# Block 0's first four feature tiles in two half blocks, a shorter weight conversion, and the first weights loaded first

## The chip, the cores and the metric

The kernel runs on one core of a Trainium2 chip. The metric is the device time of one launch in microseconds (us). Before the change it is 537.87 us, the median of three runs (537.53 to 538.58).

## What is computed

Three layers follow each other: a chunked state-space attention, a gated feed-forward layer, and a second feed-forward layer with a softmax-weighted activation.

```python
# attention, per chunk of the sequence (state starts at zero)
L = exp(cum_i - cum_j) * causal;  M = (C @ B.T) * L
y = M @ x + (C @ state) * exp(cum)
state = exp(sum(log_a)) * state + sum_j B_j x_j exp(cum_end - cum_j)
# gated layer: 3072 tokens, 256 -> 1536 -> 256
xn = x / sqrt(mean(x*x) + 1e-6) * rms_g
x  = (silu(xn @ w_gate) * (xn @ w_val)) @ w_out
# second layer: 256 -> 1024 -> 256
h = x @ w_in;  solu = h * softmax(h)
out = (solu - mean) / sqrt(var + 1e-6) * g_ln @ w_out2
```

The kernel takes the weights as the 64-bit floats that they are on the host and makes 32-bit ones of them itself.

## The kernel before, in words

**Units and blocks.** The 3072 tokens are 24 units of 128 tokens, six to each of four sequences. Four units make a block (`BLOCKS`, line 27); block 0 holds the first unit of every sequence. A unit goes through the attention (`at_...`), a block through the gated layer (`g_gate`, `g_val`, `o_mm`, lines 634 to 692), and each unit through the second layer (`m_...`).

**A unit of the attention.** `ld_bc` (line 220) and `ld_xb` (231) load it. For units 0 to 3 `at_lpe` (275) and `at_lpx` (283) make the decay matrix, `at_cb` (304) multiplies C by B, `at_mt` (314) multiplies the two on VectorE, and `at_y` (379, 384) gives the output in PSUM. Then the output is normalised: `at_sq` squares it on ScalarE (408), `at_ms` sums over partitions on TensorE (414), `at_ts` (427) and `at_pw` (432) make the inverse root, `at_rb` spreads it with a transpose against `ident` (436), `at_xc` copies the output to SBUF on ScalarE (442), `at_xn` multiplies by the gain and the inverse root on VectorE, once for each of two halves of 128 columns (447). `at_xh` (454) and `at_xl` (458) split the result into a high and a low part; `xl` ends the unit.

**The gated layer.** 1536 features are 12 tiles of 128 (`NF`). For each, `g_mm` (line 641) makes gate and value: six matmuls each (two halves of the 256 inputs, times high by high, low by high and high by low), with the block's 512 tokens as the moving columns. One PSUM bank (`pg`, `pv`) is there for each. `g_tanh` (655, ScalarE), `g_silu` (659) and `g_mul` (666, VectorE) follow. `o_mm` adds the tile into two PSUM banks `po0` and `po1`, for block 0 with one fp32 matmul per half of the outputs (686), for the others with three (689). Units 1 and 3 use `po0` and `po1` for their own products ahead of that, and the decay rows of `at_lpe` and `c_rows` (996) use `pg` and `pv`.

**Weights.** 26 pieces of 512 KB come through a ring of four staging buffers. Piece 3c is the gate weights of feature tiles 2c and 2c+1, 3c+1 the value weights, 3c+2 the output weights; the last eight are the second layer's. `w_load` (127) issues a piece on SyncE. `w_conv` makes 32-bit floats of the two 32-bit words of each number, in three operations on VectorE (135, 138, 142), `w_hi` (151, ScalarE) and `w_lo` (155, VectorE or GpSimd) split them into high and low parts.

**What sets the order.** Nothing is ordered by hand but the first instructions (lines 1136 to 1149). Every step is an `op` with an engine, a booked duration, a due time, what it comes after, and the buffers that it takes. `plan()` issues them engine by engine: among the steps that could start soonest it takes the one with the earliest due time. Each engine then runs its own list in that order. The due times come from the constants at the top (lines 28 to 53): `PRO` and `FIRST` for the start and length of block 0's gated layer, `PER` for the others, `Y0`, `YU`, `YO` for the units, `HO`, `HU` for the second layer, `EARLY` and `LEAD` for the loads. SyncE issues nearly all loads, in the planned order too.

```python
ready = [f"xl{u}" for u in range(u0, u0 + n)] if True else []
...
op(f"gm{s}", "PE", mm_us(N, 6) + 0.03, t, (g_gate, b, f), after=ready + wg_n + pr, new=[("pg", f"pg{s}")],
...
op(f"lbc{u}", "SP", 0.85, Y - 9, (ld_bc, u), new=[("bc", f"bc{u}")], kb=128)
```

So every gate of a block comes after `xl` of all its units, and a load of a unit is due a fixed time ahead of the unit.

## Time and profile before

| | before |
|---|---|
| median of the runs | 537.87 us |
| the profiled execution | 536.72 us |
| its span in the trace | 535.0 us |
| TensorE busy | 97% of the span |
| VectorE / ScalarE / GpSimd busy | 78% / 56% / 22% |
| mean granted TensorE clock | 0.990 of full speed |

The trace is of one execution; the span runs from its first to its last instruction, and the profiled execution took 1.7 us more than that. PE is TensorE, PEld its weight loads, DVE VectorE, ACT ScalarE, POOL GpSimd, SP SyncE. A name such as `pg<-xh,wg_h` says which tile is written from which.

### The profile page before, as it was taken

Reading aid. Unit: us, or ns where it says so; the run is one execution under the profiler, and the core shown is the slowest. Engines: PE = TensorE matmul, PEld = TensorE weight load, DVE = VectorE, ACT = ScalarE, POOL = GpSimd, SP = SyncE. Lnnn points to the kernel's source line nnn. Section 1 sums busy time; section 2 is a strip of 40 time slices with the busy share of each in tenths; the row PEclk is TensorE's granted clock in tenths of the full one; section 3 lists DMA queues with packets and bytes.
Section 4 is the critical chain, followed back from the end, with each engine's and each line's share of the span. In section 5 each row is a group of like instructions: output and inputs, shape, how many; then the busy total and the mean of one; then the engine's idle time right before and its main releaser. Section 6 shows DMA issues by size and latency. Waiting matters only on the chain.

```text
span 535.0 us, 9649 instructions
## 1 busy us (share of the span) xinstructions
PE 521.3 (97%) x3448; PEld 424.4 (79%) x3448; DVE 416.7 (78%) x778; ACT 301.5 (56%) x657; POOL 115.4 (22%) x147
## 2 busy tenths in 40 slices
PE   8879999999999999999999999999999999999996
PEld 8657666777878888878888888888878888888796
DVE  4889999999899897874888777797776665665674
ACT  6535544655747777763485674676534444443465
POOL 2412222531222223420131331251301000000000
PEclk9969999999999999999999999999999999999999
DMA  6672554743441643751254353253121122211200
GB/s 174 204 271 89 190 187 161 232 134 124 143 138 46 193 157 125 192 168 35 81 180 120 104 173 122 82 188 109 55 74 69 37 78 90 88 50 40 88 21 30
DMA packets 43248, 64.77 MB, mean 121 GB/s; under 512 B 7104, under 2 KB 29504, under 8 KB 43200
## 3 DMA queue, kind: packets, MB, share of 16 engines
q1 hardware_dynamic: 43200, 64.16, 38.5%
q8 instruction: 27, 0.44, 0.3%
q14 instruction: 21, 0.17, 0.1%
HBM read 50.31 MB, written 13.83 MB: 120 GB/s over the span
## 4 chain that ended last, share of the span: by engine, by line
PE 79%; DVE 10%; DMA 5%; ACT 2%; issue 2%; SPq 1%; POOL 0%; DVEq 0%; ACTq 0%; POOLq 0%
PE pg L641 16%; PE pv L641 16%; PE po L689 13%; PE pf L618 12%; PE ph L489 11%; PE po L686 3%; DMA xb<-in_xbt_dram 2%; PE y L374 2%; PE y L379 2%; PE pcb L304 1%; DMA stage<-in_wv_dram 1%; DVE wt L138 1%; PE y L414 1%; DMA stage<-in_wg_dram 1%; DVE th L659 1%
## 5 line engine op out<-in xcount | busy, mean ns | idle before, releaser
L641 PE MATMUL pg<-xh,wg_h 128*128 128x512 f32 x144 | 62.5, 434 | 1.9 <-ACT xh L454 1.2
L672 ACT ACTIVATE ah<-th 128x512 fp32r<-128x512 f32 x60 | 37.8, 629 | 47.1 <-PE po L689 31.7
L655 ACT ACTIVATE th<-pg 128x512 f32<-128x512 f32 x72 | 42.7, 593 | 30.9 <-PE pg L641 30.7
L659 DVE SCALAR_TENSOR_TENSOR th<-th,pg 128x512 f32<-128x512 f32 x72 | 49.0, 681 | 13.2 <-ACT th L655 12.9
L641 PE MATMUL pv<-xh,wv_h 128*128 128x512 f32 x144 | 58.1, 403 | 0.0
L641 PE MATMUL pg<-xl,wg_h 128*128 128x512 f32 x144 | 57.1, 397 | 0.4 <-DVE xl L458 0.4
L641 PE MATMUL pg<-xh,wg_l 128*128 128x512 f32 x144 | 57.1, 396 | 0.0
L678 DVE TENSOR_TENSOR al<-th,ah 128x512 fp32r<-128x512 f32 x56 | 41.9, 748 | 18.5 <-ACT ah L672 18.3
L641 PE MATMUL pv<-xh,wv_l 128*128 128x512 f32 x144 | 56.3, 391 | 0.0
L641 PE MATMUL pv<-xl,wv_h 128*128 128x512 f32 x144 | 56.3, 391 | 0.0
L253 ACT ACTIVATE L<-L,cneg 128x128 f32<-128x128 f32 x160 | 50.1, 390 | 3.4 <-DMA L<-crow 3.4
L618 PE MATMUL pf<-wo_h,utl 128*128 128x256 f32 x176 | 49.7, 282 | 0.6 <-DVE utl L594 0.6
L618 PE MATMUL pf<-wo_h,uth 128*128 128x256 f32 x176 | 49.6, 282 | 0.0
L618 PE MATMUL pf<-wo_l,uth 128*128 128x256 f32 x176 | 49.5, 281 | 0.0
L689 PE MATMUL po<-ah,wo_h 128*128 128x512 f32 x120 | 49.0, 408 | 0.0
L554 POOL TENSOR_TENSOR sc<-sc,mhalf 128x1 f32<-128x1 f32 x24 | 14.1, 588 | 154.9 <-DVE sc L549 154.9
L689 PE MATMUL po<-al,wo_h 128*128 128x512 f32 x120 | 47.3, 394 | 0.0
L689 PE MATMUL po<-ah,wo_l 128*128 128x512 f32 x120 | 47.3, 394 | 0.0
L666 DVE TENSOR_TENSOR th<-pv,th 128x512 f32<-128x512 f32 x60 | 41.4, 690 | 7.1 <-PE pv L641 2.0
L513 ACT ACTIVATE ut<-ph,sc 128x1024 f32<-128x1024 f32 x20 | 22.3, 1114 | 32.3 <-DVE sc L500 32.2
L489 PE MATMUL ph<-wi_h,xh 128*128 128x512 f32 x96 | 38.5, 401 | 0.3 <-DVE L L311 0.2
L489 PE MATMUL ph<-wi_h,xl 128*128 128x512 f32 x96 | 37.6, 391 | 0.2 <-DVE xl L702 0.2
(150 smaller groups left out, 1241.3 us busy)
## 6 DMA issues: line engine op xcount, KB each, us to landing
L<-crow SPq DMA_DIRECT2D x20, 512.0 KB
scr<-dt SPq DMA_DIRECT2D x20, 512.0 KB
tt<-scr SPq DMA_DIRECT2D x80, 128.0 KB
bc<-in_bcT_dram SPq DMA_DIRECT2D x48, 128.0 KB
stage<-in_wo_dram SPq DMA_DIRECT2D x10, 512.0 KB
xb<-in_xbt_dram SPq DMA_DIRECT2D x24, 192.0 KB
stage<-in_wg_dram SPq DMA_DIRECT2D x6, 512.0 KB
stage<-in_wv_dram SPq DMA_DIRECT2D x6, 512.0 KB
```

What stands on the lines that cost most here:

```text
L253: A.activation(d["L"][:, h], d["L"][:, h], AF.Exp, bias=cneg[:, R(u) * 8 + h:R(u) * 8 + h + 1])
L489: T.matmul(ph[c], xx[:, kk, k * P:(k + 1) * P], ww[:, kk, 512 * c:512 * c + 512], start=(i == 0), stop=(i == 5))
L513: A.activation(d["u"], ph[0], AF.Exp, bias=sc[:, 0:1], accum_out=sc[:, 1:2])
L618: T.matmul(d["pf"][:, 0:DM], uu[:, k], ww[:, k], start=(k == 0 and i == 0), stop=(k == 7 and i == 2))
L641: T.matmul(ps[:, :n], ww[:, kk, f * P:(f + 1) * P], xx[:, kk, :n], start=(i == 0), stop=(i == 5))
L655: A.activation(d["th"], d["pg"], AF.Tanh, scale=0.5)
L659: V.scalar_tensor_tensor(out=d["th"], in0=d["th"], scalar=1.0, in1=d["pg"], op0=ALU.add, op1=ALU.mult)
L666: V.tensor_tensor(out=out, in0=d["pv"], in1=d["th"], op=ALU.mult)
L672: A.activation(d["ah"], d["th"], AF.Copy)
L678: e.tensor_tensor(out=d["al"], in0=d["th"], in1=d["ah"].bitcast(F32), op=ALU.subtract)
L686: T.matmul(po[b, m][:, :n], w_raw(3 * (f // 2) + 2).bitcast(F32)[:, 256 * (f % 2) + m * P:256 * (f % 2) + (m + 1) * P], d["aw"], start=f == 0,
L689: T.matmul(po[b, m][:, :n], ww[:, f, m * P:(m + 1) * P], aa, start=(f == 0 and i == 0), stop=(f == NF - 1 and i == 2))
```

## The change

- The first four feature tiles of block 0 go as four half steps, numbered from `HALF` = 100. Half step `100 + 2h + j` makes feature tiles 2j and 2j+1 for units 2h and 2h+1: `h_mm` issues twelve matmuls of 256 columns for a gate, where `g_mm` issues six of 512, and puts the two tiles side by side in one bank. It comes after `xl` of its two units alone. `oh_mm` adds them to the output with two matmuls of 256 columns for each half of the outputs. From the fifth feature tile on block 0 goes as before.
- `w_conv`: the second operation was one over two tensors. Now it shifts one byte of the low word into the high word's lowest byte, in place, with byte views; the third takes its bits from the high word alone.
- `at_xc` multiplies by the gain, in two copies of 128 columns; `at_xn` is one multiplication of 256 columns. `xc` comes after `cst`, which loads the gain.
- The first two pieces are issued ahead of the plan, the first on SyncE after `aT` (the decays), the second on ScalarE's queue after `um` (the cumulation masks), which moves there from SyncE. `ident` is loaded within the plan, due at 9, and `rb` of units 0 to 3 comes after it. Loads of pieces no longer come after one another. By `EARLY` pieces 4 and 3 are due at -16.47 and -13.6, unit 0's `lbc` at 3.29 - 4.76 - 9 = -10.47.
- The constants of the due times are new, and some booked durations.

```diff
-LEAD = 17.3
-PER = (12.7, 1.36, 6.5)
+LEAD = 17.84
+PER = (12.7, 1.53, 7.29)
 WIDE = 1
+PAIRS = 2
 AHEAD = 4
-PRO = 25.1
-FIRST = 74.7
+PRO = 21.84
+FIRST = 98.91
 WARM = 7
-Y0 = (12.7, 2.9)
-YPOS = 0.58
-YSPAN = 0.85
-TAILGAP = 8.8
-SLACK = 0.15
-SLACK0 = 0.0
+Y0 = (3.29, 1.62)
+YPOS = 0.56
+YSPAN = 0.94
+TAILGAP = 12.33
+SLACK = 0.17
+SLACK0 = 0.37
...
-EARLY = (-1.0, -4.6, 2.95, 6.0)
+EARLY = (-3.25, -13.6, -16.47, 20.8)
...
-CROW = 28.3
-WGAP = 10.7
-HLAG = (52.3, 20.9)
-YO = (-2.93, 2.27, -5.8, 2.92, -2.9)
-HO = (9.9, 2.75, 0.38, 0.0, -10.0, -6.6)
-YU = (0.0, -1.59, 0.0, 0.0, 0.0, 0.0, -5.1, -5.5, 2.61, 3.5, 0.0, 0.0, 1.6, 0.0, 3.3, -7.3, 0.93, -6.4, -2.01, -0.21, 6.3, -1.89, -2.22, 0.0)
-HU = (-7.2, 0.0, 1.26, 0.0, 0.0, 0.0, 8.7, -0.65, 0.71, 0.0, 1.15, -0.74, -2.67, 1.65, -5.3, -1.89, 4.6, -1.02, 0.0, -0.82, -0.59, 8.2, 0.0, 0.0)
+CROW = 13.2
+WGAP = 13.8
+HLAG = (65.44, 23.03)
+YO = (-10.65, -4.15, -1.07, 3.02, -9.67)
+HO = (10.4, 5.84, -0.94, -3.36, -10.98, -28.16)
...
-    def w_load(i):
+    def w_load(i, e):
         src = pieces[i][1]
         t = stg[i] = sp.tile([P, 1024], I32, name="stage", tag="u", bufs=BUFS["u"])
-        S.dma_start(t.rearrange("p (k f) -> p k f", k=2), src.bitcast(I32).rearrange("(k p) f -> p k f", p=P))
+        e.dma_start(t.rearrange("p (k f) -> p k f", k=2), src.bitcast(I32).rearrange("(k p) f -> p k f", p=P))
...
         elif c == 1:
-            V.scalar_tensor_tensor(out=t, in0=v[:, :, 1], scalar=-0x40000000, in1=t, op0=ALU.bitwise_and,
-                                   op1=ALU.bitwise_or)
+            b = stg[i].bitcast(mybir.dt.uint8).rearrange("p (f w) -> p f w", w=8)
+            V.tensor_scalar(out=b[:, :, 4], in0=b[:, :, 3], scalar1=5, scalar2=None, op0=ALU.logical_shift_right)
...
             raw = w_raw(i) if pieces[i][0][0] == "o" else t
-            V.scalar_tensor_tensor(out=raw, in0=v[:, :, 0], scalar=29, in1=t, op0=ALU.logical_shift_right,
+            V.scalar_tensor_tensor(out=raw, in0=v[:, :, 1], scalar=-0x3FFFFFF9, in1=t, op0=ALU.bitwise_and,
                                    op1=ALU.bitwise_or)
...
-        A.activation(d["xts"], d["y"][:, 0:256].rearrange("p (g i) -> p g i", g=2), AF.Copy)
+        for g in range(2):
+            A.activation(d["xts"][:, g], d["y"][:, g * P:(g + 1) * P], AF.Copy, scale=rgt[:, g:g + 1])
 
     def at_xn(u):
         d = st[u]
-        for g in range(2):
-            V.scalar_tensor_tensor(out=d["xts"][:, g], in0=d["xts"][:, g], scalar=rgt[:, g:g + 1],
-                                   in1=d["y"][:, 384:512], op0=ALU.mult, op1=ALU.mult)
+        V.tensor_tensor(out=d["xts"], in0=d["xts"], in1=d["y"][:, 384:512].unsqueeze(1).to_broadcast([P, 2, P]), op=ALU.mult)
...
+    HALF = 100
...
+    def h_mm(f, ws, tag):
+        h, j = divmod(f - HALF, PAIRS)
+        ps = pp.tile([P, 512], F32, name=tag, tag=tag)
+        for q in range(2):
+            i = 0
+            for kk in range(2):
+                for xx, ww in ((xs[0][0], ws[0]), (xs[0][1], ws[0]), (xs[0][0], ws[1])):
+                    T.matmul(ps[:, 256 * q:256 * q + 256], ww[:, kk, (2 * j + q) * P:(2 * j + q + 1) * P], xx[:, kk, 256 * h:256 * h + 256],
+                             start=(q == 0 and i == 0), stop=(i == 5), skip_group_check=True)
+                    i += 1
+        act.setdefault((0, f), {})[tag] = ps
+
     def g_gate(b, f):
-        g_mm(b, f, wg_s, "pg")
+        h_mm(f, wg_s, "pg") if f >= HALF else g_mm(b, f, wg_s, "pg")
 
     def g_val(b, f):
-        g_mm(b, f, wv_s, "pv")
+        h_mm(f, wv_s, "pv") if f >= HALF else g_mm(b, f, wv_s, "pv")
...
+    def oh_mm(f, m):
+        h, j = divmod(f - HALF, PAIRS)
+        if f == HALF:
+            po[0, m] = pp.tile([P, 512], F32, name=f"po{m}")
+        for q in range(2):
+            T.matmul(po[0, m][:, 256 * h:256 * h + 256], w_raw(3 * j + 2).bitcast(F32)[:, 256 * q + m * P:256 * q + (m + 1) * P],
+                     act[0, f]["aw"][:, 256 * q:256 * q + 256], start=(f == HALF and q == 0), stop=False, skip_group_check=True)
+        if m == 1:
+            act.pop((0, f))
+
     def o_mm(b, f, m):
+        if f >= HALF:
+            return oh_mm(f, m)
...
+    FIRSTW = (S, A)
+
     def wdue(i):
         if i < 18:
             c, q = divmod(i, 3)
-            return gdue(0, 2 * c + (LAG if q == 2 else 0)) - 4.0
+            return gdue(0, (c if c < PAIRS else 2 * c) + (LAG if q == 2 else 0)) - 4.0
...
-        op(f"wl{i}", "SP", 0.45, EARLY[i] if i < len(EARLY) else t - LEAD, (w_load, i), after=[f"wl{i-1}"] if i else [], new=[("u", f"st{i}")], kb=512)
+        first = i < len(FIRSTW)
+        op(f"wl{i}", "SP", 0.0 if first else 0.45, i - 9.0 if first else EARLY[i - 2] if i < len(EARLY) + 2 else t - LEAD,
+           (int,) if first else (w_load, i, S), new=[("u", f"st{i}")], kb=512)
         for k in range(3):
-            op(f"wc{i}.{k}", "DVE", 0.41 if k == 0 else 0.68, t, (w_conv, i, k),
+            op(f"wc{i}.{k}", "DVE", 0.41 if k < 2 else 0.68, t, (w_conv, i, k),
...
+            last = [f"o{m}0.{f}" for f in ([HALF + PAIRS + c] if c < PAIRS else [2 * c, 2 * c + 1]) for m in range(2)]
...
+        steps = list(range(NF)) if b >= WIDE else list(range(HALF, HALF + 2 * PAIRS)) + list(range(2 * PAIRS, NF))
+        for g, f in enumerate(steps):
+            t = gdue(b, g)
+            to = gdue(b, g + LAG) + 2.0 if g + LAG < NF else t + 2.0 + LAG * (start[b + 1] - start[b]) / NF
             s = f"{b}.{f}"
-            pr = [f"vm{b}.{f-1}"] if f else ([f"vm{b-1}.{NF-1}"] if b else [])
-            wg_n, wv_n, wo_n = ([f"wh{3*(f//2)+q}", f"w{3*(f//2)+q}"] for q in range(3))
-            op(f"gm{s}", "PE", mm_us(N, 6) + 0.03, t, (g_gate, b, f), after=ready + wg_n + pr, new=[("pg", f"pg{s}")],
+            prev = f"{b}.{steps[g - 1]}"
+            pr = [f"vm{prev}"] if g else ([f"vm{b-1}.{NF-1}"] if b else [])
+            half = f >= HALF
+            c = (f - HALF) % PAIRS if half else f // 2
+            rdy = ready[2 * ((f - HALF) // PAIRS):][:2] if half else ready
+            wg_n, wv_n, wo_n = ([f"wh{3*c+q}", f"w{3*c+q}"] for q in range(3))
+            op(f"gm{s}", "PE", (2.6, 1.7, 1.43, 1.43)[g] if half else mm_us(N, 6) + 0.03, t, (g_gate, b, f), after=rdy + wg_n + pr, new=[("pg", f"pg{s}")],
...
+                op(f"o{m}{s}", "PE", mm_us(N, 4), to, (o_mm, b, f, m), after=[f"mu{s}", f"wc{3*c+2}.2"] + ([f"o{m}{prev}"] if g else []) + ([f"o0{s}"] if m else []),
+                   new=[(f"po{m}", f"po{m}{b}")] if g == 0 else [], use=[f"aw{s}", f"po{m}{b}", f"raw{c // 4}"])
...
+    def ld_ident():
+        S.dma_start(ident, consts[:, 3 * P:4 * P])
...
+    op("idn", "SP", 0.45, 9, (ld_ident,), kb=64)
...
-        ops[f"xn{u}"]["after"].append("cst")
+        ops[f"xc{u}"]["after"].append("cst")
+        ops[f"rb{u}"]["after"].append("idn")
...
-        SETUP = 5.2
-        free = dict(PE=SETUP, ACT=SETUP, DVE=SETUP + 0.6, POOL=SETUP, SP=2.6)
+        SETUP = 4.5
+        free = dict(PE=SETUP, ACT=SETUP, DVE=SETUP + 0.6, POOL=SETUP, SP=1.7)
...
-        S.dma_start(um, consts[:, 0:3 * P])
-        S.dma_start(ident, consts[:, 3 * P:4 * P])
+        A.dma_start(um, consts[:, 0:3 * P])
+        for i, e in enumerate(FIRSTW):
+            w_load(i, e)
```

## Rows read from the trace of the kernel before

**Rows 1.** The page, busy time of each engine.

```profile
PE 521.3 (97%) x3448; PEld 424.4 (79%) x3448; DVE 416.7 (78%) x778; ACT 301.5 (56%) x657; POOL 115.4 (22%) x147
```

**Rows 2.** Stretches, all engines: stretch, length, busy us (instructions), clock, DMA share, GB/s.

```profile
core 0: us, PE busy (x) PEld busy (x) DVE busy (x) ACT busy (x) POOL busy (x), PEclk, DMA share, GB/s
0.00:10.00 10.00, 8.49 (x58) 7.75 (x59) 3.38 (x7) 5.96 (x13) 2.07 (x8) 1.00 0.68 173
10.00:20.00 10.00, 8.67 (x119) 7.50 (x117) 7.41 (x17) 6.34 (x22) 4.20 (x8) 1.00 0.83 234
20.00:26.00 6.00, 5.12 (x61) 4.05 (x61) 5.69 (x14) 3.92 (x13) 2.89 (x4) 1.00 0.54 162
26.00:33.70 7.70, 4.59 (x33) 2.78 (x31) 6.87 (x19) 2.33 (x6) 2.63 (x3) 0.52 0.74 230
33.70:40.00 6.30, 6.30 (x21) 4.92 (x22) 5.21 (x10) 2.09 (x5) 0.00 (x0) 0.78 0.79 295
40.00:60.00 20.00, 20.00 (x137) 14.26 (x136) 18.14 (x35) 12.24 (x36) 5.09 (x5) 1.00 0.44 138
60.00:100.00 40.00, 39.73 (x290) 26.96 (x289) 38.17 (x72) 18.10 (x46) 9.82 (x10) 1.00 0.54 178
100.00:140.00 40.00, 39.37 (x293) 29.87 (x293) 37.10 (x67) 24.97 (x63) 15.16 (x18) 1.00 0.45 140
140.00:200.00 60.00, 59.73 (x403) 48.70 (x404) 54.41 (x95) 39.75 (x86) 14.89 (x21) 1.00 0.45 139
200.00:400.00 200.00, 198.87 (x1311) 166.53 (x1310) 153.52 (x284) 123.09 (x262) 51.23 (x64) 1.00 0.40 120
520.00:535.00 15.00, 10.66 (x89) 10.21 (x87) 7.07 (x24) 7.14 (x17) 1.64 (x3) 0.99 0.08 28
```

**Rows 3.** The same stretch, gate and value matmuls (line 641) alone: PE, PEld.

```profile
26.00:33.70 7.70, 0.79 (x1) 0.29 (x1) 0.52 0.74 230
```

**Rows 4.** Timeline, VectorE, low parts of units 1 and 3: start, us, instruction.

```profile
25.47 0.42 DVE L458 TENSOR_TENSOR xl<-xts,xh 128x256 fp32r<-128x256 f32 x1
...
33.23 0.42 DVE L458 TENSOR_TENSOR xl<-xts,xh 128x256 fp32r<-128x256 f32 x1
```

**Rows 5.** Chain that ended last, 0 to 110 us: start, us, what.

```profile
33.70 2.50 PE pg L641 x5
...
40.65 0.86 PE po L686 x2
41.50 1.39 PE pg L641 x6
42.89 1.36 PE pv L641 x6
```

**Rows 6.** Timeline, first 14 us: unit 0's load and matmuls, first value piece.

```profile
2.65 0.93 SPq L220 DMA_DIRECT2D bc<-in_bcT_dram  x2
...
7.94 1.16 PE L304 MATMUL pcb<-bc 16*128 16x128 f32 x16
...
13.14 0.43 DVE L135 TENSOR_SCALAR wt<-stage 128x512 int32<-128x512 int32 x1 [1.11 <-DMA stage<-in_wv_dram]
```

**Rows 7.** Chain, 300 to 330 us: 24 matmuls of 256 columns.

```profile
305.17 2.82 PE pf L618 x24
```

**Rows 8.** Lines 135, 138, 447, 442: ns min/median/max, first and last start.

```profile
L135 DVE TENSOR_SCALAR wt<-stage x26: 415/420/1526, 7.1 to 132.1; 128x512 int32<-128x512 int32 x26
...
L138 DVE SCALAR_TENSOR_TENSOR wt<-stage,wt x26: 676/693/1464, 7.5 to 132.5; 128x512 int32<-128x512 int32 x26
...
L447 DVE SCALAR_TENSOR_TENSOR xts<-xts,rgt,y x48: 330/343/348, 18.8 to 414.9; 128x128 f32<-128x128 f32 x48
...
L442 ACT ACTIVATE xts<-y x24: 365/384/387, 14.3 to 406.3; 128x256 f32<-128x256 f32 x24
```

**Rows 9.** The page, costliest groups: a dense VectorE operation of 512 columns.

```profile
L659 DVE SCALAR_TENSOR_TENSOR th<-th,pg 128x512 f32<-128x512 f32 x72 | 49.0, 681 | 13.2 <-ACT th L655 12.9
```

**Rows 10.** Stretches, second conversion operation (line 138) alone: VectorE.

```profile
20.00:26.00 6.00, 0.68 (x1) 1.00 0.54 162
26.00:33.70 7.70, 1.36 (x2) 0.52 0.74 230
```

More of the change, by code (lines that the diff above doesn't have):

```diff
@@ L763, in fused_kernel @@
             ops[f"wc{i}.2"]["use"] += wu
-            last = [f"o{m}{b}.{2 * c + q}" for b in range(WIDE) for q in range(2) for m in range(2)]
+            last = [f"o{m}0.{f}" for f in ([HALF + PAIRS + c] if c < PAIRS else [2 * c, 2 * c + 1]) for m in range(2)]
         op(f"wh{i}", "ACT", 0.63, t, (w_hi, i), after=[f"wc{i}.2"], use=wu)
@@ L872, in fused_kernel @@
         ready = [f"xl{u}" for u in range(u0, u0 + n)] if True else []
[L873 to L875 removed]
+        steps = list(range(NF)) if b >= WIDE else list(range(HALF, HALF + 2 * PAIRS)) + list(range(2 * PAIRS, NF))
+        for g, f in enumerate(steps):
+            t = gdue(b, g)
+            to = gdue(b, g + LAG) + 2.0 if g + LAG < NF else t + 2.0 + LAG * (start[b + 1] - start[b]) / NF
             s = f"{b}.{f}"
[L877 to L879 removed]
+            prev = f"{b}.{steps[g - 1]}"
[5 more added lines that the diff above has]
+            op(f"gm{s}", "PE", (2.6, 1.7, 1.43, 1.43)[g] if half else mm_us(N, 6) + 0.03, t, (g_gate, b, f), after=rdy + wg_n + pr, new=[("pg", f"pg{s}")],
                use=[f"pg{s}", f"xs{b}"])
[L881 removed]
+            op(f"vm{s}", "PE", (2.0, 1.6, 1.42, 1.42)[g] if half else mm_us(N, 6) + 0.015, t, (g_val, b, f), after=[f"gm{s}"] + wv_n, new=[("pv", f"pv{s}")],
                use=[f"pv{s}", f"xs{b}"])
@@ L889, in fused_kernel @@
             for m in range(2) if wide else ():
-                op(f"o{m}{s}", "PE", mm_us(N, 4), to, (o_mm, b, f, m), after=[f"mu{s}", f"wc{3*(f//2)+2}.2"] + ([f"o{m}{b}.{f-1}"] if f else []) + ([f"o0{s}"] if m else []),
-                   new=[(f"po{m}", f"po{m}{b}")] if f == 0 else [], use=[f"aw{s}", f"po{m}{b}", f"raw{f // 8}"])
+                op(f"o{m}{s}", "PE", mm_us(N, 4), to, (o_mm, b, f, m), after=[f"mu{s}", f"wc{3*c+2}.2"] + ([f"o{m}{prev}"] if g else []) + ([f"o0{s}"] if m else []),
+                   new=[(f"po{m}", f"po{m}{b}")] if g == 0 else [], use=[f"aw{s}", f"po{m}{b}", f"raw{c // 4}"])
             if wide:
```

18 lines of the change are left out of this document (8 added, 10 removed).

## The prediction

> **What bounds the kernel now.** I read the page's busy shares first: TensorE is busy for 97% of the span [rows 1]. Then the stretches, to see where it is not [rows 2]: from 33.7 to 400 us it stands idle for 2.3 us in all, so nothing there can be won but by giving it less work. The loss lies ahead of 33.7 us. Between 26 and 33.7 TensorE is busy for 4.59 us out of 7.70, at a granted clock of 0.52, close to the lower of its two levels (1.2 GHz); 0.79 us of that is one gate matmul that was issued and then waited [rows 3]. So 3.80 us of other work stand in 7.70 us, ahead of hundreds of us of dense work. Third, what that time waits for: the second unit's low part (line 458) ends at 25.47 + 0.42 = 25.9 us, the fourth unit's at 33.23 + 0.42 = 33.65 us [rows 4], and block 0's first gate runs from 33.70 us [rows 5], because its matmuls are 512 columns wide and want all four units. Last, what paces the units: from 20 to 33.7 us VectorE is busy for 12.56 of 13.7 us, while in the first 20 us it is idle for 9.2 [rows 2], partly because it waits for weights that were issued late: the first value piece, issued behind the units' loads, keeps it waiting 1.11 us, until 13.14 us [rows 6].
>
> So a lead that TensorE wins ahead of 33.7 us stays to the end, if VectorE can follow. From 20 to 100 us VectorE is idle for only 5.9 us of 80 [rows 2]; this cover has to be checked for each part.
>
> **Half blocks.** The first four feature tiles of block 0 become four half steps: tiles 0,1 and 2,3 for units 0,1, then the same for units 2,3. The first half step may start when unit 1 is done, at 25.9 instead of 33.65 us by the times of before: 7.8 us earlier. The gap is not all free: the 3.80 us of unit work in it stay. They ran at the low clock, so at full clock they are between 1.9 us (half) and 3.80 us. How much of it is at which clock? In before the first gate took 2.50 us against 1.39 later [rows 5]; a mean clock of 0.78 over the 6.30 us from 33.7 [rows 2] means about 2.8 us at the low level after the gates begin. I take that price as the same wherever the gates begin: it is then paid once in both kernels and cancels, and some two thirds of the unit work runs at full clock; I take 2.4 us for it. The lead is 7.8 - 2.4 = 5.4 us (bounds from the unit work alone: 4.0 and 5.9).
>
> Is there enough to fill it? Two half steps hold two gates and two values, four times 1.41 us (twelve matmuls of 256 columns, at 2.82 / 24 = 0.1175 us each [rows 7]), 5.6 us. That covers 5.4 us, barely; the output matmuls can't help, since units 1 and 3 use their two PSUM banks until they are finished. A unit 1 that comes earlier still thus gives nothing more; only an earlier unit 3 does.
>
> Twice as many gate and value matmuls of half the width cost 8 x (1.41 - 1.39) = 0.16 us; the 16 output matmuls in place of 8 have no row at that width. Proportional to columns they cost nothing more, and if each of the 8 added ones cost a whole matmul of before, 0.43 us [rows 5], it is 3.4 us. The gates kept to columns within 2%, so I take 0.24. Together -0.4 us.
>
> **Shorter conversion.** Each of 26 pieces had three VectorE operations on 512 elements: one of 0.42 us with one tensor operand, two of 0.69 us with two [rows 8]. The second becomes a one-operand shift on single bytes, read and written every 8 bytes. No row shows a byte operation. The bounds are 0.42 us, the one-operand row, and 1.46 us, the longest of the two-operand ones [rows 8]. I take 0.42, since line 135 has the same element count, one operand and the same read stride; it saves 0.27 x 26 = 7.0 us of VectorE ahead of 140 us. The third operation keeps form and size. The normalisation (line 447) goes from 2 x 0.34 us [rows 8] to one operation of 256 columns; line 458 has that width at 0.42 [rows 4], so 0.26 us less per unit. ScalarE gets two scaled copies of 128 columns for one of 256; they cost between nothing more and 0.38 us more per unit, as if each half took what the whole did [rows 8]. ScalarE is busy for 2.33 of 7.70 us in the tight stretch [rows 2], and the copy is wanted only after the squares, the mean, the power and the transpose. I cost it at nothing; without that cover it is 1.5 us over four units.
>
> None of this is TensorE time. It pays for the lead: TensorE 5.4 us ahead wants VectorE's work 5.4 us sooner, out of 5.9 us of idle time from 20 to 100 us, plus 0.27 for each piece and 0.26 for each unit there. That fits, even if the byte operation saves nothing. What it may give beyond is part of the 1.2 us for which TensorE is idle between 60 and 200 us [rows 2]: +0.6, bounds 0 and 1.2.
>
> **Loads.** The first gate piece leaves SyncE right behind the decays, the first value piece leaves ScalarE's queue behind the cumulation masks. Two more pieces, value 1 and gate 1, have due times of -16.47 and -13.6, ahead of unit 0's first load at -10.47, so they go out before it on SyncE. Before, that load was issued at 2.65 us, and its matmuls ran at 7.94 [rows 6]. Now 2.39 MB (four pieces of 512 KB, 192 KB, 96 KB) stand ahead of or beside it. At 295 GB/s (33.7 to 40 us) that is 8.1 us, at 234 GB/s (10 to 20 us) 10.2 [rows 2]: counted from 0.8 us, unit 0's operands land between 8.9 and 11.0 us, 1 to 3 us late. What is gained is that VectorE can convert four pieces in its 9.2 idle us before 20 instead of between 20 and 33.7, where it did three [rows 10] at 0.42 + 2 x 0.69 us, 5.4 us. The two may go either way; unit 3 may end 2.7 us sooner (half of the 5.4) or 3.1 us later. I take the times of before: 0. Two issues on ScalarE's queue take about 2 x 0.47 us (half of a pair on SyncE [rows 6]) ahead of its first logarithm, which waits for the decays anyway: 0, and at most 0.9. The identity's load moves behind these; its first reader is unit 0's transpose, the last matmul of that unit: 0, by the same delay as above at most.
>
> **Retimed order.** Nearly every due time is new, the tail's spacing too. The trace shows only what there is to win: 1.1 us idle from 200 to 400, and in the last 15 us 4.3, most of which is the drain of the last unit [rows 2]. To lose there is no bound in it. I take 0.
>
> Sum: -5.4 + 0.4 - 0.6 = -5.6 us. The profiled execution took 536.72 us (span 535.0), 1.15 below the median of the runs, 537.87; the sum makes 531.1 of it, and taken from the median **532.3 us**.
>
> **Rivals.**
> 1. *The units come late and eat the lead.* The loads above delay units 1 and 3 by d, and VectorE, 92% busy from 20 to 33.7 us, does not catch up: gain 5.6 - d, for d of 3.1 us 535.4. For it: the bytes. Against: the idle time of VectorE before 20 us. Chance 0.12. In the first 10 us the 16 DMA engines are 0.68 busy [rows 2], so they have some room. The Trainium skill, DMA: Bandwidth & Descriptors, "Issuing engines are not separate DMA queues", says that transfers from several issuing engines share the same 16 engines and interleave, and that only issue time is saved. By that rule the first value piece slows the unit's loads although it leaves on another queue, and the sum is that of this rival; no row here has two queues at work to show it.
> 2. *The byte operation is the new bound* (the other side). If byte access every 8 bytes costs 1.46 us, the conversions up to 140 us grow by 26 x 0.77 = 20.0 us. VectorE has 8.8 us idle from 20 to 140 [rows 2], saves about 2.5 in normalisation, and regains perhaps 3 of the early idle time: 20.0 - 14.3 = 5.7 us slower, 543.6. It decides from 0.69 + 14.3 / 26 = 1.24 us on. For it: no row shows a strided write. Against: the strided reads of line 138 cost no more than dense operations of its kind, 0.69 against 0.68 us [rows 8, 9]. Chance 0.05. The Trainium skill, Vector Engine (DVE) Microarchitecture Reference, "Measured stream behaviour on trn2", has a port fall below its full rate when successive words are not adjacent pairs, down to 2.5 ns per column for a destination in small hops. An estimate from that page is 512 x 2.5 ns = 1.3 us for the byte operation, by which the sum would be some 1.6 us slower than before; the trace disagrees for reads, with 0.42 us for 512 hopping elements in line 135.
> 3. *The halves don't start early.* TensorE works in order; if a matmul of units 2 or 3, or a PSUM bank that the decay rows still hold, stands ahead of the first half gate, it starts near 33.7 us as before: 537.9, within 0.2%. Chance 0.05.
> 4. *The new order opens stalls later on*, for instance weights due later behind a ring of four staging buffers, worth more than the lead: about 540. Chance 0.03.
>
> **How the numbers follow.** The forecast has 0.75. Its best case is a unit 3 that ends 2.7 us sooner (8.1), all of the 1.2, and 0.3 of cost: 9.0 us, 528.9; I go to 528.3, since TensorE idles 1.3 us between 10 and 20 us as well, which earlier units could shorten [rows 2]. The range reaches up to 536.0, which holds most of rival 1, and leaves out rivals 2 to 4 (0.13) and some 0.07 at its ends. Faster by over 0.2% (1.1 us, about what a measurement of this kernel can tell from no change): 0.75 + 0.12 = 0.87; within it 0.05; slower 0.08.
>
> **What would show it.** Right: the first gate near 25 us and no gap of TensorE until unit 3; the byte operation near 0.42 us; TensorE's idle time after 40 us no larger. Wrong: unit 0's first matmuls well after 8 us with all else shifted; a byte operation over 0.7 us; gates that wait for VectorE between 40 and 100 us.

## The result, and the profile after

The changed kernel takes 546.85 us in the median (542.86 to 548.87, four runs) against 537.7 of the kernel before in the same session: 1.0147 times as long, 95% interval 1.0113 to 1.018. The forecast was 532.3 and faster; it is 9.2 us slower, and 14.6 us off the forecast. The execution shown below took 548.87 us, the slowest of the four; its span is 547.1, 12.1 more than before.

The page, busy time of each engine in the changed kernel:

```profile
PE 526.9 (96%) x3512; PEld 437.4 (80%) x3512; DVE 418.9 (77%) x743; ACT 307.4 (56%) x681; POOL 131.5 (24%) x158
```

Nothing stands out against [rows 1]: VectorE is busy for 2 us more, GpSimd for 16. The loss is in the stretches (the same columns as [rows 2]):

```profile
0.00:10.00 10.00, 8.24 (x42) 7.86 (x42) 2.38 (x5) 5.99 (x15) 1.88 (x8) 1.00 0.84 289
10.00:20.00 10.00, 8.21 (x84) 7.35 (x85) 9.75 (x16) 5.31 (x16) 5.80 (x7) 0.87 0.74 198
20.00:26.00 6.00, 6.00 (x61) 5.32 (x61) 2.62 (x8) 3.49 (x12) 1.58 (x3) 0.65 0.48 126
26.00:33.70 7.70, 7.02 (x71) 5.62 (x73) 7.07 (x15) 3.17 (x10) 4.99 (x7) 0.83 0.43 118
33.70:40.00 6.30, 5.62 (x61) 5.26 (x58) 5.55 (x13) 3.27 (x8) 1.05 (x2) 0.94 0.88 267
40.00:60.00 20.00, 19.01 (x163) 17.21 (x162) 18.21 (x33) 11.63 (x34) 4.94 (x5) 0.91 0.53 178
60.00:100.00 40.00, 35.43 (x274) 25.37 (x272) 36.77 (x60) 17.41 (x48) 15.57 (x13) 0.96 0.57 185
100.00:140.00 40.00, 34.80 (x180) 24.69 (x184) 36.86 (x60) 20.02 (x50) 11.44 (x11) 0.96 0.30 89
140.00:200.00 60.00, 60.00 (x437) 49.23 (x437) 45.68 (x78) 36.32 (x82) 14.40 (x17) 1.00 0.31 94
200.00:400.00 200.00, 200.00 (x1330) 167.72 (x1329) 155.71 (x280) 132.47 (x289) 60.19 (x72) 1.00 0.45 137
```

From 40 to 140 us TensorE is idle for 0.99 + 4.57 + 5.20 = 10.8 us, where it was idle for 0.9 before; and the granted clock, 1.00 all through that time before, is 0.91, 0.96 and 0.96, which costs, by an estimate from the share not granted, another 0.09 x 20 + 2 x 0.04 x 40 = 5.0 us. Together that is 14.9 us more than before. Ahead of 40 us the same sum (idle time, and the part of the clock not granted) is 10.0 us against 11.9, and from 140 to 400 TensorE saves the 1.4 us for which it idled before. Net 11.6 us of the 12.1. So the front became a little better, and what it won was lost several times over behind it, in block 0's gated layer. After 140 us nothing is lost. The 5.0 us are those of this execution, whose mean granted clock is 0.981; the fastest of the four, at 0.990, took 542.86 us.

The timeline of the first 33 us, as in [rows 4] and [rows 6]: first issues, unit 0's matmuls, low parts of units 0 and 1, the copies of the decay rows (`ct`), the fourth unit's C times B, first half gate.

```profile
1.24 0.46 ACTq L128 DMA_DIRECT2D stage<-in_wv_dram  x1
...
2.72 0.93 SPq L221 DMA_DIRECT2D bc<-in_bcT_dram  x2
...
10.32 1.39 PE L305 MATMUL pcb<-bc 16*128 16x128 f32 x16 [1.03 <-DMA bc<-in_bcT_dram]
...
23.26 0.42 DVE L458 TENSOR_TENSOR xl<-xts,xh 128x256 fp32r<-128x256 f32 x1 [0.54 <-ACT xh L454]
...
27.68 0.44 DVE L1033 COPY ct<-pc 96x256 f32<-96x256 f32 x1
28.06 0.58 DVE L458 TENSOR_TENSOR xl<-xts,xh 128x256 fp32r<-128x256 f32 x1
...
28.95 0.41 DVE L1033 COPY ct<-pc 96x256 f32<-96x256 f32 x1
...
29.63 1.16 PE L305 MATMUL pcb<-bc 16*128 16x128 f32 x16
30.72 0.39 PE L653 MATMUL pg<-xh,wg_h 128*128 128x256 f32 x1
```

Unit 0's load is issued almost when it was (2.72 against 2.65 us), but its matmuls run at 10.32 instead of 7.94, since its bytes land later. Unit 1's low part is 2.6 us late, and the first half gate starts at 30.72, 3.0 us ahead of the old first gate and not the 7.8 that stood in the prediction. The copies that free the gates' two banks run at 27.68 and 28.95 us although the decay rows are due at 13.2 in this plan; in the kernel before, due at 28.3, they ran at 26.48 and 27.41. Here the second bank is free at 29.36 us, and the gate follows the fourth unit's C times B, which runs until 30.8.

The operations of [rows 8] in the changed kernel, by source line (ns min/median/max, first and last start):

```profile
L136 DVE TENSOR_SCALAR wt<-stage x26: 414/420/1516, 8.2 to 122.0; 128x512 int32<-128x512 int32 x26
...
L140 DVE TENSOR_SCALAR stage<-stage x26: 727/754/1720, 9.1 to 122.4; 128x512 uint8<-128x512 uint8 x26
...
L448 DVE TENSOR_TENSOR xts<-xts,y x24: 408/414/423, 22.3 to 423.4; 128x256 f32<-128x256 f32 x24
...
L444 ACT ACTIVATE xts<-y,rgt x48: 352/364/379, 16.7 to 420.0; 128x128 f32<-128x128 f32 x48
```

The byte operation takes 0.75 us, neither the 0.42 of the forecast nor the 1.46 of the upper bound: 0.06 more than the operation that it replaces. The estimate of 1.3 us from the Trainium skill, Vector Engine (DVE) Microarchitecture Reference, "Measured stream behaviour on trn2", whose rows are for four-byte words, is off on the other side, by 0.55 us against 0.33. The normalisation costs VectorE 0.27 us less per unit, as forecast; each half copy on ScalarE takes 0.36 us, nearly what the whole one took (0.38), so close to the upper bound.

The chain that ended last, 40 to 140 us: shares of this stretch by line (each 1% is 1 us), and three of its pieces.

```profile
by line: DVE stage L140 12.2%; DMA L<-crow 10.7%; issue 8.0%; DVE wt L136 7.3%; DVE wt L143 7.2%; PE pv L642 5.5%; DVE th L672 4.9%; PE po L714 4.2%; DVE aw L679 3.6%; DVE xl L458 3.5%; PE pg L642 2.8%; DMA bc<-in_bcT_dram 2.8%; DVE wv_l L1
...
63.15 1.45 DVE wt L136
64.63 1.70 DVE stage L140
66.33 1.26 DVE xl L458
```

The same row of the kernel before begins with TensorE's gates, values and outputs (lines 641, 686 and 689), 56.1% of the stretch:

```profile
by line: PE pv L641 19.1%; PE pg L641 19.0%; PE po L686 14.4%; PE pcb L304 6.8%; DVE wt L138 3.9%; PE po L689 3.6%; PE y L374 3.4%; DMA stage<-in_wv_dram 3.4%; issue 2.9%; PE y L379 2.6%; DVE th L659 2.4%; DVE wt L142 2.1%; DVE xl L458 1.9%
```

After the change they are a small part, and VectorE's weight conversion (lines 136, 140, 143) alone is 26.7 us. The second entry of the chain after the change is not VectorE's: two loads of decays for later units (`L<-crow`, pieces of 5.0 and 5.7 us, the first begun at 36.54 us). What TensorE itself waits for from 40 to 140 us (total, times, longest) are the last four rows here, and they make up the whole 10.8 us. The first row is a wait of ScalarE, ahead of that in the second:

```profile
ACT xts L444 <- DVE s L396: 10.2, 3, 4.2
...
PE y L415 <- ACT xts L444: 4.9, 3, 2.4
...
PE y L415 <- DVE sq L423: 3.3, 1, 3.3
...
PE pg L642 <- DVE th L672: 1.6, 1, 1.6
...
PE pg L653 <- DVE th L672: 1.0, 1, 1.0
```

So 2.6 us are waits for gated tiles (`th`). The larger part, 8.2 us, are waits of the units: the sum over partitions (`at_ms`, L415), which has its place among the gates in TensorE's list, waits for the scaled copy on ScalarE (L444) or for a sum of squares on VectorE (L423), and the copy waits for the unit's state update on VectorE (L396). VectorE comes to these late, behind conversions and gated tiles in its list. In the kernel before TensorE's waits in this stretch are 0.9 us in all.

Three pieces of the chain show a second thing, in the timeline of VectorE and GpSimd:

```profile
62.96 1.35 POOL L156 TENSOR_TENSOR wg_l<-wt,wg_h 128x512 fp32r<-128x512 f32 x1 [0.55 <-ACT wg_h L152]
63.08 1.52 DVE L136 TENSOR_SCALAR wt<-stage 128x512 int32<-128x512 int32 x1
...
64.27 3.03 POOL L156 TENSOR_TENSOR wo_l<-wraw,wo_h 128x512 fp32r<-128x512 f32 x2
64.63 1.70 DVE L140 TENSOR_SCALAR stage<-stage 128x512 uint8<-128x512 uint8 x1
66.12 1.47 DVE L458 TENSOR_TENSOR xl<-xts,xh 128x256 fp32r<-128x256 f32 x1
...
69.49 0.28 DVE L396 SCALAR_TENSOR_TENSOR s<-s,e,y 128x64 f32<-128x64 f32 x1
```

While GpSimd makes low parts of weights, three VectorE operations whose usual times are 0.42, 0.75 and 0.42 us take 1.52, 1.70 and 1.47. The state update at 69.49, for which the copy waited 4.2 us, comes behind them. The changed order puts 13 of the 22 low parts of this kind on GpSimd, the old one 7. That alone doesn't set the changed kernel apart: the same kernel with a truer booking, further down, has 14 there and is 9 us faster.

### The profile page after: what moved, and what is told of

Same layout as the page of the kernel before. It is cut to its first block, busy times and chain, and to the rows that moved or that the text cites. A ratio compares the mean times of both kernels' runs of the same rounds, so it can differ in the third digit from the quotient of the medians.

```text
span 547.1 us, 9807 instructions
## 1 busy us (share of the span) xinstructions
PE 526.9 (96%) x3512; PEld 437.4 (80%) x3512; DVE 418.9 (77%) x743; ACT 307.4 (56%) x681; POOL 131.5 (24%) x158
## 4 chain that ended last, share of the span: by engine, by line
PE 79%; DVE 11%; DMA 4%; ACT 2%; issue 2%; SPq 1%; DVEq 0%; ACTq 0%
PE po L714 16%; PE pv L642 15%; PE pg L642 15%; PE pf L618 13%; PE ph L489 12%; DVE stage L140 3%; DMA L<-crow 2%; DVE wt L136 2%; PE y L375 2%; PE y L380 2%; DVE wt L143 2%; DMA stage<-in_wv_dram 1%; PE pcb L357 1%; PE y L415 1%; PE pg L653 1%
## 5 line engine op out<-in xcount | busy, mean ns | idle before, releaser
L642 PE MATMUL pg<-xh,wg_h 128*128 128x512 f32 x136 | 57.0, 419 | 1.6 <-DVE th L672 1.6
L642 PE MATMUL pv<-xh,wv_h 128*128 128x512 f32 x136 | 55.5, 408 | 0.0
L642 PE MATMUL pv<-xh,wv_l 128*128 128x512 f32 x136 | 54.1, 398 | 0.0
L642 PE MATMUL pv<-xl,wv_h 128*128 128x512 f32 x136 | 54.0, 397 | 0.0
L642 PE MATMUL pg<-xh,wg_l 128*128 128x512 f32 x136 | 53.7, 395 | 0.0
L642 PE MATMUL pg<-xl,wg_h 128*128 128x512 f32 x136 | 53.4, 393 | 0.0
L691 DVE TENSOR_TENSOR al<-th,ah 128x512 fp32r<-128x512 f32 x47 | 33.1, 705 | 21.6 <-ACT ah L685 21.3
L489 PE MATMUL ph<-wi_l,xh 128*128 128x512 f32 x96 | 37.5, 391 | 0.0
```

The lines of the kernel that those rows point to most:

```text
L489: T.matmul(ph[c], xx[:, kk, k * P:(k + 1) * P], ww[:, kk, 512 * c:512 * c + 512], start=(i == 0), stop=(i == 5))
L642: T.matmul(ps[:, :n], ww[:, kk, f * P:(f + 1) * P], xx[:, kk, :n], start=(i == 0), stop=(i == 5))
L691: e.tensor_tensor(out=d["al"], in0=d["th"], in1=d["ah"].bitcast(F32), op=ALU.subtract)
```

## The experiments

Each time stands beside runs of the kernel before on the same chip; ratios are to it, with 95% intervals. Between kernels that ran on different chips a difference of ratios, times 537.6 us, is the safer number, and "by the ratios" means that. "The half block kernel" is the kernel before with the half blocks, their output step and their places in the plan taken from the change, and with the decay rows due early; it is run first without the latter.

### What the byte operation costs

**The changed order, with the operation that the plan booked.** The plan books the second conversion operation at 0.41 us. A copy of the first operation takes that long.

```diff
-            V.tensor_scalar(out=b[:, :, 4], in0=b[:, :, 3], scalar1=5, ...
+            V.tensor_scalar(out=t, in0=v[:, :, 1], scalar1=3, scalar2=0x3FFFFFF8, op0=ALU.logical_shift_left, op1=ALU.bitwise_and)
```

> The changed kernel with its byte operation (0.75 us, against 0.42 booked by the plan) replaced by a second copy of the first conversion operation (0.42 us), in the same place of the same order on every engine; the lowest three bits of the weights are then not right. Theory A (price): VectorE was late between 45 and 140 us because 26 byte operations cost 0.33 us more than booked, and more beside GpSimd (0.88 us mean there); with 19 of them in that stretch at 0.42, some 9 us come back: 534 to 538.5 us. Theory B (order): the new due times put weight pieces of later layers ahead of block 0's own work, whatever a conversion costs: 543 us or more.

539.09 us, ratio 1.0021 (1.0002 to 1.0039), 7.8 us below the changed kernel, 6.8 by the ratios: theory A, though 0.6 us above its range. The source line of this operation, then the stretches:

```profile
L139 DVE TENSOR_SCALAR wt<-stage x26: 415/427/1379, 8.3 to 113.5; 128x512 int32<-128x512 int32 x26
```

```profile
60.00:100.00 40.00, 36.43 (x265) 25.63 (x256) 37.95 (x68) 19.87 (x54) 14.99 (x14) 1.00 0.62 195
100.00:140.00 40.00, 35.95 (x240) 26.68 (x239) 33.25 (x59) 19.78 (x50) 9.75 (x10) 1.00 0.26 86
```

26 x 0.33 = 8.6 us less on VectorE give 6.8 us of time: in this order most of a microsecond of VectorE ahead of 140 us is time of the kernel. Every engine's list is the same as in the changed kernel, so no other order can be behind the difference. The clock is at 1.00 in this execution, but 7.6 us of idle time are left in these two rows, and the time is still no better than before.

**The byte operation in the order of before.** The kernel before with the new conversion alone, all bookings untouched.

> The kernel before with the new conversion alone (byte operation and new third operation), all else and the order as before. Theory A: 26 operations of 0.75 in place of 0.69 us, +1.6 us on VectorE of which half is hidden: 538 to 540 us; up to 542 if the byte operation stretches more beside GpSimd than the old one did. Theory B: 537.5 to 539 us. Forecast of the prediction's second rival (1.24 us or more each): above 538 by its size, 543.

540.34 us, 1.0045 (1.0021 to 1.007). The same length as in the changed kernel, by its source line:

```profile
L139 DVE TENSOR_SCALAR stage<-stage x26: 729/749/1519, 7.3 to 136.1; 128x512 uint8<-128x512 uint8 x26
```

26 x 0.06 = 1.6 us more on VectorE, and some 2.4 us slower. By itself the "shorter" conversion is a loss in this order, a small one.

**No second operation at all,** in the changed order and in the order of before; the mask of the third operation then clears the three lowest bits.

> The changed kernel without the second conversion operation: the lowest three bits of the weights are zero. Order as changed. Theory C (VectorE decides between 45 and 140 us, so that each us taken off it there comes back): after 0.75 to 0.42 gave 7.8 us, 0.42 to nothing (another 0.43 x 19 = 8 us in that stretch) gives at least 4 more: 531 to 535 us, below the kernel before. Theory D (with the booked price the order itself holds TensorE up, by loads and waits): no more than 2 us more, 537 to 540.

> The kernel before without the second conversion operation (lowest three bits of the weights zero), order as before: 26 x 0.69 = 18 us less VectorE work ahead of 140 us. Theory C: VectorE paces the units ahead of 33.7 us too, with five of the operations there, so the first gate comes 2 to 3 us sooner and TensorE's 4 us of losses from 40 to 140 shrink by half: 532 to 535 us. If the order fixed for the old price leaves the time where other waits hold it: 536 to 538 us.

The changed order: 531.22 us, 0.9895 (0.9859 to 0.9931), 15.6 us below the changed kernel (13.5 by the ratios) for some 19.5 us less on VectorE. The order of before: 535.89 us, 0.9977 (0.9942 to 1.0011), so 18 us less on VectorE give nothing that the interval tells from no change. So most of VectorE's time is hidden in the old order and hardly any of it in the changed one.

### Is it the operation, or its booking?

The plan lays out every engine's list with booked times. The byte operation is booked at 0.41 and takes 0.75.

```diff
-            op(f"wc{i}.{k}", "DVE", 0.41 if k < 2 else 0.68, t, (w_conv, i, k),
+            op(f"wc{i}.{k}", "DVE", (0.41, 0.75, 0.68)[k], t, (w_conv, i, k),
```

> The changed kernel with the byte operation's booked duration set to what it takes (0.75 in place of 0.41 us); nothing else, so only the planned order moves. If the loss is the mismatch between plan and chip (theory A1), the planner finds an order for the true price and most of the 8 us come back: 537 to 541 us. If it is the work itself on a full VectorE (theory A2), little comes back, or the due times fit the new order worse: 544 us or more.

537.56 us, 1.0012 (0.9977 to 1.0047): with the same work, 9.3 us below the changed kernel, 7.3 by the ratios. Its stretches, 40 to 140 us:

```profile
40.00:60.00 20.00, 20.00 (x168) 17.54 (x167) 19.09 (x34) 12.07 (x34) 8.10 (x8) 1.00 0.60 196
60.00:100.00 40.00, 36.74 (x281) 25.06 (x280) 38.33 (x65) 17.93 (x47) 13.60 (x12) 1.00 0.53 175
100.00:140.00 40.00, 38.80 (x251) 28.67 (x250) 36.83 (x66) 24.31 (x62) 13.36 (x13) 1.00 0.37 116
```

The idle time falls from 10.8 to 4.5 us. Part of the 9.3 us goes with the granted clock, which differs between executions of one and the same kernel. Where it is alike the two kernels are 3.0 us apart (542.86 against 539.87 us, both at 0.990), or 4.3 and 6.3 (545.68 against 541.36 at 0.984, 548.87 against 542.59 at 0.981).

With the conversion of before, booked as before (0.68), the changed kernel should then be about as fast:

> The changed kernel with the old conversion, booked at its old durations, all else as changed. The byte operation booked at its true 0.75 gave 537.6. If the 0.06 us between them are all: 536 to 537.5. If half blocks, loads and new due times together are worth the lead once the conversion is right: 532 to 535. If booking, and not price, was what the changed kernel lacked, as the last run says, it is no better than that one: 537 to 539.

538.85 us, 1.0026 (0.9989 to 1.0063). It is. Two more prices, 0.65 and 0.85, ask whether the cost follows the size of the miss:

> The changed kernel with the byte operation booked at 0.65 us, 0.10 below its measured 0.75 (booked at 0.75 it took 537.6 us, at 0.41 546.9). Theory (the miss of the booking is what costs, some 9 us for 0.34): 538 to 541. Rival (the nine microseconds are what one order happens to be worse than another, and every small change of a price makes a new order): anywhere from 533 to 547, not in line with the size of the miss.

> The same with the operation booked at 0.85, 0.10 above its measured time. Theory (a booking too long does not put work late, so it costs little): 536 to 540. Rival (any new order can be good or bad): anywhere from 533 to 547; the span of this run, the run before and 537.6 is then the scatter of orders that no booking explains.

535.02 us, 0.9974 (0.9934 to 1.0014), and 539.52 us, 1.0048 (1.0016 to 1.0081). The first was expected at 538 to 541 and missed: 0.10 too short is no worse than right. Each price gives another order, and the four whose prices are within 0.10 us of the measured times lie between 0.9974 and 1.0048, a scatter of 4.0 us; the changed kernel, 0.34 short, lies at 1.0147, and its interval begins (1.0113) above where all of theirs end (1.0081). So small misses drown in the scatter from order to order, and the one large miss tried on this kernel stands out of it; that the cost grows with the miss is not shown.

A price that is too high was also tried the other way round, on the changed kernel without the operation: the plan told that it is gone (0.085 in place of 0.41).

> The changed kernel without the second operation of the conversion (the three lowest bits of each weight stay zero), with the plan told so: booked at 0.085 instead of 0.41. As booked at 0.41 it took 531.2 us. Theory (the plan's price matters in both directions): 527 to 530. Rival (it matters only where work is late, not where it is early): 530 to 532.

536.12 us, 0.9953 (0.9919 to 0.9986), against 531.2 as booked too long. A miss for the theory: the truer price made it 3.1 us slower by the ratios, though the intervals overlap a little. That a booking is true is no promise of a good order; what the runs show is only that an operation booked far too short costs, here and in one more kernel below.

### What the half blocks give

**Half blocks alone,** all due times of before.

> The kernel before with half blocks alone: conversion, normalisation, loads, constants and booked durations as before. Theory A: no byte operation, so the lead of the half blocks shows: 531 to 535 us. Theory B says the same. A third view, that half blocks are worth nothing because VectorE has no room for gates ahead of unit 3: 537 us or more.

537.89 us, 1.0014 (0.9991 to 1.0036): nothing. The timeline tells why:

```profile
25.99 0.42 DVE L459 TENSOR_TENSOR xl<-xts,xh 128x256 fp32r<-128x256 f32 x1
...
32.42 0.74 DVE L1031 COPY ct<-pc 96x256 f32<-96x256 f32 x2
...
32.89 0.58 PE L654 MATMUL pg<-xh,wg_h 128*128 128x256 f32 x1 [1.06 <-DVE ct L1031]
```

Unit 1 is done at 26.4 us, but the half gate waits for the copy of the decay rows out of PSUM, which comes only at 32.4. **With the decay rows due early,** as the change has them:

```diff
-CROW = 28.3
+CROW = 13.2
```

> The kernel before with half blocks, and the decay rows (which hold the gates' two PSUM banks) due at 13.2 in place of 28.3. With half blocks alone the first half gate began at 32.9 us, not at 26, behind the decay rows' copies. If only that held the lead back: first half gate at 26 to 28 us, and 532 to 535 us. If VectorE has no room to follow (theory C): TensorE starts early and waits later, between 45 and 140 us, 536.5 to 539 us.

532.84 us, 0.9926 (0.99 to 0.9952). The first half gate starts at 28.91, a little later than expected, since unit 1's low part now runs at 28.82, and the stretches keep what is won:

```profile
26.00:33.70 7.70, 7.70 (x59) 6.62 (x58) 5.23 (x15) 4.09 (x11) 3.06 (x4) 0.50 0.53 180
...
60.00:100.00 40.00, 39.25 (x248) 27.59 (x247) 38.47 (x71) 19.25 (x50) 14.63 (x17) 1.00 0.59 192
100.00:140.00 40.00, 40.00 (x308) 31.20 (x307) 37.97 (x72) 24.45 (x57) 9.79 (x12) 1.00 0.41 131
```

TensorE is never idle from 26 to 33.7 us, and for 0.75 us from 60 to 140. By the ratio that is 2.6 to 5.4 us won.

**And the normalisation** of the change added:

> Half blocks with the decay rows early (532.8 us before) and the changed normalisation: two scaled copies on ScalarE, one multiplication on VectorE, with their booked durations. Forecast of the prediction: 0.26 us of VectorE less per unit (2 us up to 140 us), nothing lost: 531 to 533 us. If the order, planned anew with due times made for neither, decides by chance: anything within 3 us of 532.8.

535.2 us, 0.9953 (0.9927 to 0.998). The forecast of 531 to 533 is missed; VectorE's saving gives nothing that the intervals tell.

**And the conversion without its second operation,** booked so:

> Half blocks with the decay rows early, without the second conversion operation (lowest three bits of the weights zero), and the plan told so. Theory C (VectorE paces the units and the stretch to 140 us): both gains add, 532.8 - 1.5 to 4: 528.5 to 531.5 us. If the lead is all that there is to win: 532 to 533.

530.69 us, 0.9871 (0.9826 to 0.9915), as expected: by the ratios 3.0 us below the half block kernel, though the intervals overlap.

**And the byte operation, booked at 0.41 and at 0.75** (work and due times the same in both):

> The half block kernel with the decay rows early (532.8 us) and, beside it, the byte conversion booked at 0.41 as the change books it; loads, normalisation and due times untouched. Theory (an operation that takes 0.34 us longer than its booking puts the planned orders of the engines out of step): 537 to 542, with over 3 us of TensorE idle between 40 and 140 us. Rival (the wrong price matters only in the order that the change's due times make): 532 to 535, as the same kernel with the true price, and at most 1 us idle.

> As the run before, with the byte operation booked at its measured 0.75 us. The byte operation takes 0.06 us more than the operation it replaces, 1.6 us of VectorE in all. Theory: 532 to 536, within 1.5 us of the kernel without it (532.8), and 3 us or more below the run before. Rival: equal to the run before within 1 us.

539.3 us, 1.0024 (0.9994 to 1.0054), against 530.8 us, 0.9855 (0.9806 to 0.9903). The price in the plan alone is worth 8.5 us (9.1 by the ratios), with the loads of before and, but for the decay rows, its due times. The stretches, booked short:

```profile
60.00:100.00 40.00, 36.74 (x235) 25.10 (x235) 36.02 (x71) 19.03 (x50) 10.63 (x10) 1.00 0.53 167
100.00:140.00 40.00, 39.05 (x255) 29.56 (x253) 37.13 (x66) 19.59 (x44) 9.57 (x10) 1.00 0.43 141
```

and booked right:

```profile
60.00:100.00 40.00, 39.85 (x295) 28.11 (x294) 36.59 (x66) 18.57 (x48) 18.89 (x19) 1.00 0.59 183
100.00:140.00 40.00, 40.00 (x263) 31.01 (x262) 37.99 (x73) 23.07 (x53) 9.27 (x9) 1.00 0.44 145
```

VectorE is about as busy in both; TensorE is idle for 4.2 us in the first, 3.0 of it behind gated tiles, and 0.15 in the second. That is half of the difference; in these two executions most of the rest lies ahead of 40 us, where idle time and clock not granted come to 9.6 and 5.4 us. The clock doesn't tell the two kernels apart: it is 0.987 to 0.997 in the ten executions of the first and 0.993 to 0.997 in the four of the second. **This last kernel does all of the work and beats both.** That it is 2 us below the half block kernel, with 1.6 us more work on VectorE, and below the range of the theory, is within the scatter of orders.

### Loads and due times

**The first loads of the change in the half block kernel.**

```diff
+        A.dma_start(um, consts[:, 0:3 * P])
+        for i, e in enumerate(FIRSTW):
+            w_load(i, e)
```

> Half blocks with the decay rows early and the two first loads as changed (first piece right behind the decays, second on ScalarE's queue with the masks, the identity within the plan). Forecast of the prediction: 0, between -2.7 and +3.1 us: 530 to 536. By its first rival the unit's first operands land later than at 7.9 us, and half gates with them: 534 to 536. More than 540 would put the 551 us of the changed kernel with old constants down to the loads.

541.91 us, 1.0073 (1.0037 to 1.0108), 7.9 us above the half block kernel by the ratios, and above both the forecast and the rival. Its stretches:

```profile
60.00:100.00 40.00, 37.49 (x236) 26.43 (x235) 36.82 (x72) 18.60 (x49) 14.43 (x14) 0.96 0.55 181
100.00:140.00 40.00, 37.30 (x245) 27.55 (x244) 32.96 (x58) 19.99 (x50) 9.17 (x9) 1.00 0.26 85
```

Unit 0's matmuls run at 12.30 us in it, and the first half gate at 30.61; but the larger loss is again behind 60 us, with 5.2 us of idle time in these two rows. No operation is booked far too short here, so that an unlucky order alone may be worth this much: this run can't tell the early bytes from the order that the plan made with them.

**The due times of before in the changed kernel.**

> The changed kernel with all due-time constants of the kernel before (piece 2 and 5 due at 2.95 and 6.0, pieces 3 and 4 by their rule); half blocks, conversion, normalisation and the two first loads as changed. Theory A: the byte operation still costs 0.75, so VectorE is late as well: 541 us or more. Theory B: the old due times bring the order back, 537 us or less.

551.35 us, 1.0252 (1.0218 to 1.0287). With the old due times the change is slower still; beside its loads and its wrong booking the new ones save 5.6 us by the ratios.

**The changed kernel with the byte operation booked right, and the loads as before.**

> The changed kernel with the byte operation booked at 0.75 (537.6 us as it stood, TensorE idle for 4.46 us between 40 and 140 us), and with the first loads as before: pieces 0 to 3 issued on SyncE in the order of before, the masks and the identity ahead of the plan on SyncE. Theory (the first loads cost the lead, as they did in the half block kernel: 541.9 against 532.8): 532 to 535, first C times B near 7.9 us, first half gate before 28 us, idle below 2 us in 40 to 140. Rival (the new due times want the new loads; what is lost there is the order's, not the loads'): 537 to 540, no less idle time.

535.93 us, 0.9963 (0.9939 to 0.9987): 2.6 us by the ratios below the same with the new loads, and the two intervals overlap. The first C times B runs at 7.12 us and the first half gate at 26.33, as the theory has it, and 2.4 us are idle from 40 to 140; but the time lies between the two forecasts. With the new due times the early loads cost little, if anything; with the old ones the same edit costs 7.9 us.

## Why the prediction was wrong

**The step that failed** is in the part on the conversion, in two sentences. "I take 0.42" was mis-sized: 0.75 us, and the 7.0 us of VectorE that it was to save are a cost of 1.6. A later sentence would have covered that, "That fits, even if the byte operation saves nothing", and it is this one that decided. It compared sums of VectorE work with sums of its idle time, as if the work could move into the gaps. It can't: each engine runs a list fixed beforehand, laid out with the byte operation at 0.41 us, and each conversion that ends 0.34 us late delays what stands behind it, the units' state updates and squares as well as the gated tiles, and TensorE waits for these. 26 such delays are 8.8 us; by the ratios 6.8 come back at the booked length with the order kept, 7.3 with the right booking, and 9.1 in the half block kernel. Of the miss of 14.6 us the first two are about half, and less (3.0 to 6.3 us) where the granted clock is alike. The other half is the gain that was forecast and that the changed kernel doesn't show even when it is booked right. The prediction knew of the booked durations; the diff has 0.41 for the new operation beside two operations whose booking agrees with their measured time, and the bounds of 0.42 and 1.46 should have been put against that booking, not only against the idle sum.

**Rival 2**, the byte operation as the new bound, came true in its sign with a price of 0.75 us, far below the 1.24 from which it was to decide. The threshold was the error, by the same reckoning of sums. But its mechanism, a price too high for VectorE, is not what the runs show: booked at its price, the same operation leaves the changed kernel where the kernel before is (1.0012).

**"Loads: I take the times of before: 0"** failed as well. Rival 1 foresaw unit 0 1 to 3 us late, and it was 2.4: 10.32 against 7.94 us, with the load issued at the same time. By the rule that it cites from the Trainium skill, DMA: Bandwidth & Descriptors, "Issuing engines are not separate DMA queues" (transfers of several issuing engines share the same 16 engines), it was to be so. The trace agrees, but as three of the four pieces ahead of the load are SyncE's own, it doesn't show the part of the other queue by itself. But the price of the new loads is not only that delay. With the due times of before the edit costs 7.9 us, most of it behind 60 us; whether the early bytes do that or the order that comes with them isn't shown.

**Half blocks: right in size, wrong in what stands in the way.** The forecast was -5.4 + 0.4 = -5.0 us; the half block kernel gives -2.6 to -5.4. It needs the decay rows out of the bank first, which is rival 3, seen in the run without them moved. The change has the early due time, but its order still copies them at 27.68 and 28.95 us. What comes late there as well is unit 1's low part, at 28.06. In the profile after, the lead is spent by 60 us: it is 1.9 us at 40 us, and 2.8 go between 40 and 60.

**Normalisation:** VectorE's saving per unit came as forecast and gave no time. ScalarE's second copy was costed at nothing, with 0.38 us per unit if the cover is gone; it takes 0.34. In the changed kernel TensorE waits 4.9 us behind this copy from 40 to 140 us, so the cover was gone there; but the copy itself waited 10.2 us for VectorE's state update, so this too goes back to a late VectorE. The run that adds this part alone to the half block kernel shows no difference that its interval can tell; no run takes it out of the changed one.

**Retimed order: "I take 0".** The prediction saw no bound for a loss here, and that was so: the new orders lost 7 to 9 us by one wrong price, and orders with nearly the same prices differ by 4. What it did not do is to widen the range for that: 536.0 was its upper end.

**Open** is why the changed kernel, booked right and with the loads of before, is at 535.9 and not at the 530.8 of the half block kernel with the same conversion: its normalisation, its other due times and booked durations, or the scatter of orders, which is nearly as large. So is what sets the scatter.

## What to carry to other kernels

Where a planner fixes each engine's order, an edit has two prices: what an operation takes, and what the plan believes that it takes; look at both in the diff and measure the new operation before it is booked. Idle time added up over a long stretch is no cover for an engine that is busy for over 90% of it and that others wait for: ask in which row of the chain the delay stands, and count it there in full. Orders made with nearly the same prices differ by some 4 us here, and the early loads' by 8, so that a part's gain of that size needs more than one order to be believed.

## What the runs showed of the hardware

- A VectorE shift on 512 single bytes per partition, 8 bytes apart, in place, takes 0.75 us, where a shift on 512 words of four bytes with the same 8-byte step takes 0.42.
- VectorE operations of 0.42 to 0.75 us took 1.5 to 1.7 us in the lines shown, beside GpSimd's low parts of 512 columns. No run changes this alone.
- The granted clock was 0.91 and 0.96, between its two levels, in the stretches of block 0 in which TensorE waited, an estimated 5.0 us beside the 10.8 of waiting; at the booked length of the operation it stayed at 1.00 there, with 8.5 us of waiting. So the waiting alone doesn't explain it.
- It also differs between executions of one kernel with one order: of 25 executions of the kernel before in one session, six at 0.981 took 540.1 to 541.4 us, sixteen at 0.989 and above 536.1 to 538.0. What lowers it isn't shown.
